# Linear attention and two feed-forward layers in one kernel: running products on (-im, re, im) words, state products in 32-column tiles, a third place for the accumulators' copies, shared places for squares

## The chip, the core and the metric

The kernel runs on one core of a Trainium2 chip. TensorE (PE in the profile) does the matrix products, VectorE (DVE) and ScalarE (ACT) the elementwise work, SyncE (SP) starts the transfers. Each of these engines works off its own queue in order. The metric is the time of one execution on the device in microseconds; the smaller the better.

## The reference, cut to what matters

```python
def _attn_ref(q, k, v, a_re, a_im):          # (4, 8, 768, 48) each
    mag = np.sqrt(a_re * a_re + a_im * a_im)
    scale = np.minimum(mag, 0.999) / (mag + 1e-06)
    a_re_n, a_im_n = (a_re * scale, a_im * scale)
    for t in range(S):
        S_re, S_im = a_re_n*S_re - a_im_n*S_im + k v^T, a_re_n*S_im + a_im_n*S_re
        y[:, :, t] = einsum('bhd,bhde->bhe', q[:, :, t], S_re)

def _moe_ref(x, w_in, w_out):                # 3072 x 384, d_ff 2048
    h = x @ w_in
    return (h * (1.0 / (1.0 + np.exp(-1.702 * h)))) @ w_out

def _moe2_ref(x, w_gate, w_val, w_out):      # d_ff 1536
    g = x @ w_gate
    return (g * (1.0 / (1.0 + np.exp(-g))) * (x @ w_val)) @ w_out

# result: _moe2_ref(_moe_ref(attention's y as 3072 x 384))
```

A linear attention with a complex decay for each key dimension and time step, for 4 batches and 8 heads, then two feed-forward layers over the 3072 tokens. The weights come as 64-bit floats and are converted in the kernel.

## The kernel before

**Attention.** The 768 steps of a batch are cut into chunks of 128, and two chunks make a *unit*: 4 batches x 3 units = 12 units, numbered from 0. For a unit the decays (`u.p`, 128 partitions x real and imaginary part x 768 words) are loaded (`load_a`), squared and summed (`decays`: `sq`, `m2`), brought to scale with a reciprocal root (`root`, ScalarE's Ln and Exp, another function table than the one for Gelu), and multiplied into `u.p` (`scale_pair`). `products` then makes running products over time in place: within each group of 8 steps one complex product after another (`cmul`: one multiply of 4 x 96 words into `sp`, a subtract and an add of 96 words each, lines 390, 397, 399; seven such steps a unit), then over groups of 4 and again 4 (`bq`, `hh`), over the chunks (`G`), and last the prefixes `e` are multiplied into all words (`prod`, line 454). `queries` and `keys` multiply q by the running product and k by its inverse (`inverse`, again Ln and Exp), write them to memory and `load_heads` reads them back by heads (`sq`, `sk`). `turns` transposes the keys on TensorE (`kt`, `kn`). `heads` makes for each chunk the masked scores (`sc`, `at`), the outputs (`y`, 32-column tiles, four of them side by side in the array), and the state's gain (`ds`, line 676: for each of 8 heads one product with 96 columns of weights and 48 moving columns, each in two passes since the words are 32 bits wide); `split_x` leaves y as a high and a low half in `xt`.

**First layer.** `layer_one` multiplies each unit's `xt` with 16 blocks of w_in (`h`, nine products a block, lines 846 to 848), `gelu` follows on ScalarE and VectorE, `layer_one_out` multiplies with w_out into one accumulator of three parts (`acc`), and after a unit's sixteenth block `spill` copies the three parts out on ScalarE (line 944) and sends them to memory (`x2d`). There is one accumulator (`accslots`), so the next unit's first `acc` product waits until the third copy is done. The copies go to tiles named `stage`, of which there are two; a tile is free again when its transfer has landed.

**Second layer.** Blocks of 512 tokens: `pg`, `pv`, silu, `o`. Its weights are converted while the last units of the first layer run.

**What sets the order.** `Plan` is a list scheduler that runs when the kernel is built: each step is a generator that yields events, places (`Slots`) and requests for an engine with an assumed duration; the planner takes what is ready first, with a table of urgencies (`URGENCY`, `EXTRA`, `NEAR`, `W_FIRST`, `SPILL`...), and the instructions go into the engines' queues in that order, which is then fixed. The number of places of each kind is in `BUFS`: four tiles `p`, two tiles `big` (squares, queries, `prod`), one each of `m2`, `x`, `d2`.

Of the kernel before, what the change touches and what calls it, by code (L numbers as in the profile page):

```python
# [185 lines left out]
NEAR = 0.068  # L186
# [7 lines left out]
NEAR0 = [0.129, 0.072]  # L194
# [3 lines left out]
class Attention:  # L198
# [46 lines left out]
    BUFS = dict(p=4, big=2, m2=1, r=1, x=1, d2=1, kr=1, qk=2, v=1, s=1, kn=1, at=2, m=2, sc=2, xt=2, tots=1)  # L245
# [6 lines left out]
    def start(self, units):  # L252

        add = self.plan.add
        for i, (b, c0, n) in enumerate(units):
            u = type("Unit", (), {})()
            u.i, u.b, u.c0, u.n, u.F, u.T, u.t0 = i, b, c0, n, n * self.HD, n * 128, c0 * 128
            u.urgency = {nm: URGENCY[nm] + 10 * i + (EXTRA[i].get(nm, 0) if i < len(EXTRA) else 0) for nm in URGENCY}
            u.near = NEAR0[i] if i < len(NEAR0) else NEAR
            u.ev = {e: Event() for e in ("a", "l", "lv", "q", "k", "v", "m2", "root", "scaled", "prods", "d2", "inv", "qh", "dq", "dk",  # L260
                                        "sq", "sk", "tots", "kn", "x", "phase")}
            u.kn = {}
            u.turned = [Event() for _ in range(n)]
            self.units.append(u)
        for u in self.units:
            last = self.units[u.i - 1] if u.i else None
            for nm, row in (("a", self.load_a(u)), ("l", self.load_qkv(u)), ("d", self.decays(u)),
                            ("p", self.products(u, last)), ("q", self.queries(u)), ("k", self.keys(u)),
                            ("r", self.root(u)), ("i", self.inverse(u)), ("s", self.load_heads(u)), ("t", self.turns(u)), ("h", self.heads(u, last))):
                add(u.urgency[nm], row, near=u.near)  # L270


    def load_a(self, u):
        yield self.slots["p"]
        yield ISSUE2
# [27 lines left out]
    def decays(self, u):  # L303
# [5 lines left out]
        yield slots["m2"]  # L309
# [7 lines left out]
        plan.give(slots["big"])  # L317
        plan.set(u.ev["m2"])
        yield u.ev["root"]
        yield slots["x"]  # L320
        yield act(u.F, more=0.11)
        x = self.tile("x", [128, self.NT, u.T])
# [6 lines left out]
        plan.give(slots["m2"])  # L329
# [7 lines left out]
        plan.give(slots["x"])  # L337
        yield from self.scale_pair(u, u.p, u.r)
        plan.give(slots["r"])
        plan.set(u.ev["scaled"])  # L340
# [30 lines left out]
    def cmul(self, out, x, y, shape):  # L371

        V = self.nc.vector
        n = 1
        for s in shape:
            n *= s
        if len(shape) == 2:
            full = [128, 2] + list(shape)
            for c in range(2):
                yield vec(2 * n)  # L380
                if c == 0:
                    p = self.sb.tile([128, 2, 2, n], F32, tag="sp", name="sp", bufs=2)
# [3 lines left out]
        else:  # L386
            full = [128, 2, 2] + list(shape)
            yield vec(4 * n, 0.3 if n > 48 else 0.0)
            p = self.sb.tile([128, 2, 2, n], F32, tag="sp", name="sp", bufs=2)
# [11 lines left out]
    def products(self, u, last):  # L401
# [5 lines left out]
        pf = u.p.rearrange("p e j (b r) -> p e (j b) r", r=8)  # L407
# [3 lines left out]
        p7 = pf[:, :, :, 7].rearrange("p e (i k) -> p e i k", k=4)  # L411
# [34 lines left out]
        h = g * 16 // n  # L446
        for c in range(n):
            yield slots["big"]
            pv = pf[:, :, cols(c, h)]
            for i in range(2):  # L450
                yield vec(16 * h)
                if i == 0:
                    prod = self.tile("big", [128, 2, 2, h, 8], name="prod")
                V.tensor_tensor(out=prod[:, i], in0=eb[:, i:i + 1, cols(c, h), None].to_broadcast([128, 2, h, 8]), in1=pv,
                                op=ALU.mult)
            yield from self.add_parts(pv, prod, 8 * h)
            plan.give(slots["big"])
        plan.set(u.ev["prods"])
# [71 lines left out]
    def keys(self, u):  # L530
# [3 lines left out]
        yield slots["d2"]  # L534
# [4 lines left out]
        u.d2 = self.tile("d2", [128, self.NT, u.T])  # L539
        V.scalar_tensor_tensor(out=u.d2, in0=sq[:, 0], scalar=1 / BIG / 2 ** 64, in1=sq[:, 1], op0=ALU.max, op1=ALU.add)  # L540
        plan.give(slots["big"])
# [6 lines left out]
        plan.give(slots["d2"])  # L548
# [75 lines left out]
    def heads(self, u, last):  # L624
# [12 lines left out]
        for c in range(u.n):  # L637
# [87 lines left out]
URGENCY = dict(a=-2808.9, d=-847.7, p=-2094.7, r=-3052.8, i=4533.3, q=1516.2, k=-385.1, t=-1239.2, h=76.9, g=-110.3, s=3227.3, l=-328.4, m=-5154.4, x=-1279.9)  # L725
RUSH = 3154.3
RUSH2 = -1700.0
EXTRA = [dict(a=-2098.5, d=-2358.9, p=1710.8, r=-2037.7, i=-2834.0, q=-3757.0, k=-2737.4, t=2298.5, h=973.7, g=-1739.2, s=3534.0, l=8424.0, m=-93.5, x=-1732.5), dict(a=-1805.4, d=1780.9, p=-1232.5, r=-16347.3, i=5601.4, q=-10544.3, k=1608.0, t=-2254.4, h=-1967.0, g=-7019.6, s=-12442.9, l=-9458.0, m=-2831.4, x=3813.5), dict(a=6291.4, d=11280.8, p=-1463.1, r=7217.9, i=-10027.3, q=3231.8, k=2532.1, t=-10835.3, h=-6846.7, g=-312.0, s=-4214.7, l=6684.3, m=-11385.8, x=-3197.1), dict(a=2012.2, d=4387.5, p=299.7, r=-1602.7, i=-86.2, q=6261.4, k=1243.8, t=-1886.3, h=-1311.3, g=-11850.9, s=-3015.3, l=10131.5, m=-5199.2, x=-7519.5), dict(a=-3194.7, d=-6390.0, p=-96.6, r=-3467.8, i=1530.6, q=2540.9, k=-2099.8, t=-5418.7, h=-2426.8, g=-2422.7, s=-767.9, l=-3000.5, m=-5411.6, x=1182.2), dict(a=-1050.3, d=-144.2, p=806.6, r=1424.0, i=139.9, q=-166.2, k=3312.5, t=856.6, h=458.2, g=-4074.4, s=-362.2, l=4171.4, m=-99.2, x=393.5), dict(a=-7427.0, d=5500.1, p=594.0, r=-3662.6, i=725.5, q=-7111.1, k=615.3, t=778.1, h=416.6, g=2162.2, s=-112.0, l=-593.1, m=-1297.8, x=1878.2), dict(a=111.4, d=5462.3, p=1433.9, r=-4618.4, i=24.5, q=3526.1, k=2232.0, t=1785.0, h=-462.5, g=-670.7, s=-71.3, l=-2330.6, m=-2800.1, x=-2443.0), dict(a=-523.3, d=-1120.5, p=-1956.2, r=583.7, i=-4090.9, q=-3868.4, k=-2787.2, t=-4123.6, h=-7130.2, g=1607.9, s=-71.9, l=1329.4, m=-748.8, x=332.7), dict(a=3903.2, d=4589.9, p=1692.7, r=1460.9, i=2272.8, q=1521.7, k=-692.3, t=185.5, h=477.9, g=-6354.1, s=49.3, l=5191.9, m=-1557.4, x=2485.8), dict(a=1214.6, d=-838.8, p=335.0, r=2129.7, i=3251.8, q=-1710.9, k=-2147.3, t=-560.4, h=150.2, g=2186.9, s=1499.3, l=1080.2, m=-2407.0, x=-1150.2), dict(a=-355.1, d=3117.9, p=4624.6, r=-5461.8, i=586.7, q=2689.3, k=-6.4, t=-1989.6, h=-3324.0, g=-682.7, s=4777.1, l=9171.0, m=684.6, x=-1889.2)]
UNITS = [(b, c, 2) for b in range(4) for c in (0, 2, 4)]
W_FIRST, W_STEP = 2068.1, 12.097  # L730
# [3 lines left out]
SPILL = -2740.5  # L734
# [7 lines left out]
def chunked(ctx, tc, keep, dram, q, k, v, a_re, a_im, w_in, w_out, w_gate, w_val, w_out2, out):  # L742
# [31 lines left out]
    stage, rough, junks, wslots = Slots(2), Slots(ROUGH), Slots(1), Slots(2 * F1)  # L774
# [163 lines left out]
    def spill(u, acc):  # L938
        N = u.T
        for c in range(KT):  # L940
            yield stage
            yield act(N, more=-0.05)
            x2 = raw.tile([128, N], F32, tag="stage", name="x2", bufs=2)
# [377 lines left out]
```

## Time and profile before

| | us |
|---|---|
| median of 3 runs (1146.59 to 1150.03) | 1147.72 |
| the profiled execution | 1151.18 |
| its span, first to last instruction | 1149.5 |
| PE busy | 1060.9 (92%) |
| DVE busy | 729.6 (63%) |
| ACT busy | 557.1 (48%) |
| mean granted TensorE clock | 0.962 |

A profile holds one execution. Views used here: the busy time of each engine in stretches of the span (with the granted clock), the table of who waited for whom, the instructions in order of time, and the groups by line. In a row of instructions in time, the first number is the start in microseconds from the span's start, the second the time until the last of the row's instructions ended, then engine, line, operation, result and sources, shapes, and the count; in brackets the idle time of the engine before it, with what ended it. An instruction of DVE or ACT overlaps the next one's start by some tenths of a microsecond, so what it costs its engine is read from start to start.

### The profile page before, as it was taken

Reading aid. Unit: us, or ns where it says so; the run is one execution under the profiler, and the core shown is the slowest. Engines: PE = TensorE matmul, PEld = TensorE weight load, DVE = VectorE, ACT = ScalarE, POOL = GpSimd, SP = SyncE. Lnnn points to the kernel's source line nnn. Section 1 sums busy time; section 2 is a strip of 40 time slices with the busy share of each in tenths; the row PEclk is TensorE's granted clock in tenths of the full one; section 3 lists DMA queues with packets and bytes.
Section 4 is the critical chain, followed back from the end, with each engine's and each line's share of the span. In section 5 each row is a group of like instructions: output and inputs, shape, how many; then the busy total and the mean of one; then the engine's idle time right before and its main releaser. Section 6 shows DMA issues by size and latency. Waiting matters only on the chain.

```text
span 1149.5 us, 19994 instructions
## 1 busy us (share of the span) xinstructions
PE 1060.9 (92%) x7968; PEld 968.7 (84%) x7968; DVE 729.6 (63%) x1646; ACT 557.1 (48%) x1297; POOL 7.5 (1%) x23
## 2 busy tenths in 40 slices
PE   2549988999999999989999999999999999999996
PEld 0228878899999999889999998888888888888885
DVE  6899999999989986898962899432232222312221
ACT  8897565853575547644453999221121222211211
POOL 2000000000000000000000000000000000000000
PEclk9759998999999999899999999999999999999998
DMA  9750634326634246014633680110010010000000
GB/s 335 254 151 29 153 97 124 101 71 189 171 100 113 87 112 179 15 60 107 165 96 81 203 302 23 28 38 17 1 55 1 15 42 1 28 1 1 29 1 30
DMA packets 92182, 103.60 MB, mean 90 GB/s; under 512 B 4785, under 2 KB 86194, under 8 KB 92082
## 3 DMA queue, kind: packets, MB, share of 16 engines
q1 hardware_dynamic: 92082, 102.26, 30.9%
q8 instruction: 64, 1.05, 0.4%
q14 instruction: 36, 0.29, 0.1%
HBM read 73.93 MB, written 28.31 MB: 89 GB/s over the span
## 4 chain that ended last, share of the span: by engine, by line
PE 74%; DVE 11%; DMA 9%; ACT 4%; issue 1%; SPq 1%; DVEq 0%; ACTq 0%
PE o L1070 4%; PE o L1071 4%; PE o L1072 4%; PE pg L847 4%; PE acc L846 4%; PE h L846 4%; PE pv L847 4%; PE pv L846 4%; PE pg L848 4%; PE pg L846 4%; PE pv L848 4%; PE acc L847 4%; PE acc L848 4%; PE h L848 4%; PE h L847 4%; PE sc L616 4%
## 5 line engine op out<-in xcount | busy, mean ns | idle before, releaser
L1040 DVE TENSOR_TENSOR s<-s,pv 128x512 f32<-128x512 f32 x72 | 49.5, 687 | 243.0 <-PE pv L848 241.8
L846 PE MATMUL acc<-gs,w 128*128 128x256 f32 x576 | 169.4, 294 | 14.8 <-ACT x L944 14.8
L846 PE MATMUL h<-xt,w 128*128 128x256 f32 x576 | 169.1, 294 | 4.9 <-ACT g L902 4.9
L847 PE MATMUL acc<-gs,w 128*128 128x256 f32 x576 | 166.2, 289 | 0.3 <-DVE gs L908 0.3
L848 PE MATMUL acc<-gs,w 128*128 128x256 f32 x576 | 166.0, 288 | 0.0
L848 PE MATMUL h<-xt,w 128*128 128x256 f32 x576 | 164.7, 286 | 0.5 <-ACT w L836 0.5
L847 PE MATMUL h<-xt,w 128*128 128x256 f32 x576 | 164.7, 286 | 0.1
L900 ACT ACTIVATE gs<-h 128x256 fp32r<-128x256 f32 x192 | 74.1, 386 | 151.3 <-PE h L848 150.5
L846 PEld LDWEIGHTS acc<-gs,w 128*128 128x128 f32 x576 | 113.6, 197 | 15.8 <-ACT x L944 15.6
L1037 ACT ACTIVATE s<-pg 128x512 f32<-128x512 f32 x72 | 43.1, 599 | 166.8 <-PE pg L848 166.8
L846 PEld LDWEIGHTS h<-xt,w 128*128 128x128 f32 x576 | 112.6, 196 | 8.0 <-ACT g L902 6.6
L847 PEld LDWEIGHTS acc<-gs,w 128*128 128x128 f32 x576 | 113.7, 197 | 0.6 <-DVE gs L908 0.5
L848 PEld LDWEIGHTS acc<-gs,w 128*128 128x128 f32 x576 | 113.6, 197 | 0.0
L847 PEld LDWEIGHTS h<-xt,w 128*128 128x128 f32 x576 | 112.5, 195 | 0.3 <-DVE xt L719 0.3
L848 PEld LDWEIGHTS h<-xt,w 128*128 128x128 f32 x576 | 112.1, 195 | 0.7 <-ACT w L836 0.7
L908 DVE TENSOR_TENSOR gs<-g,gs 128x256 fp32r<-128x256 f32 x192 | 81.0, 424 | 49.5 <-ACT g L902 48.8
L1045 ACT CAST p<-s 128x512 fp32r<-128x512 f32 x72 | 44.8, 622 | 133.5 <-DVE s L1040 133.4
L1070 PE MATMUL o<-w,p 128*128 128x384 f32 x288 | 97.2, 338 | 0.0
L1071 PE MATMUL o<-w,p 128*128 128x384 f32 x288 | 97.2, 337 | 0.0
L1072 PE MATMUL o<-w,p 128*128 128x384 f32 x288 | 97.2, 337 | 0.0
L847 PE MATMUL pg<-xs,w 128*128 128x512 f32 x216 | 85.1, 394 | 0.0
L847 PE MATMUL pv<-xs,w 128*128 128x512 f32 x216 | 84.7, 392 | 0.0
(137 smaller groups left out, 2316.6 us busy)
## 6 DMA issues: line engine op xcount, KB each, us to landing
words<-in_moe_w_out_dram SPq DMA_DIRECT2D x28, 384.0 KB, 8.4
dq<-qh SPq DMA_DIRECT2D x24, 384.0 KB, 4.1
sq<-dq SPq DMA_DIRECT2D x24, 384.0 KB, 6.7
dk<-p SPq DMA_DIRECT2D x24, 384.0 KB, 5.0
sk<-dk SPq DMA_DIRECT2D x24, 384.0 KB, 5.1
words<-in_moe_w_in_dram SPq DMA_DIRECT2D x16, 384.0 KB, 8.5
p<-in_a_re_dram SPq DMA_DIRECT2D x12, 384.0 KB, 3.8
p<-in_a_im_dram SPq DMA_DIRECT2D x12, 384.0 KB, 4.6
```

The costliest lines, as they stand in the source:

```text
L616: T.matmul(sc[:, h], u.sk[:, 4 * g + h, cols(c)], u.sq[:, 4 * g + h, cols(c)], start=True, stop=True)
L846: T.matmul(out, w[:, 0, ws], xh, start=start, stop=False)
L847: T.matmul(out, w[:, 0, ws], xl, start=False, stop=False)
L848: T.matmul(out, w[:, 1, ws], xh, start=False, stop=stop)
L900: A.activation(gs[:, 0], h, AF.Gelu_apprx_sigmoid)
L908: V.tensor_tensor(out=gs[:, 1], in0=g, in1=gs[:, 0].bitcast(F32), op=ALU.subtract)
L1037: A.activation(s, gv[0], AF.Silu)
L1040: V.tensor_tensor(out=s, in0=s, in1=gv[1], op=ALU.mult)
L1045: A.copy(p2[:, 0], s)
L1070: T.matmul(os[i], p2[:, 0, cols(i)], w[:, 0], start=f == 0, stop=False)
L1071: T.matmul(os[i], p2[:, 0, cols(i)], w[:, 1], start=False, stop=False)
L1072: T.matmul(os[i], p2[:, 1, cols(i)], w[:, 0], start=False, stop=f == F2 - 1)
```

## The change

Four edits and a new table of urgencies.

1. **Running products.** Scaled decays are no longer written back into `u.p` but into a tile `tri` (`u.w`) of three words for each element, (-im, re, im); VectorE writes re and im, ScalarE copies -im. One step is then a multiply of 384 words with (re, im) and (-im, re) as pairs, and a single add of 192 words. The last multiply (`prod`) reads `tri` and writes a new `u.p`. `sp` has one tile instead of two.
2. **State products.** Each of the 8 heads' `ds` products becomes three with 32 columns, to three places of the array.
3. **Spill.** `stage` has three tiles instead of two.
4. **Places.** `m2`, `x` and `d2` are halves of the `big` tile that holds the squares, which is given back later; `big` has three tiles, `p` three instead of four. `load_a` waits for the unit before and for the products of the third unit before. Scaling a unit waits for the products of the one before, since there is one `tri`.

```diff
-    BUFS = dict(p=4, big=2, m2=1, r=1, x=1, d2=1, kr=1, qk=2, ...)
+    BUFS = dict(p=3, tri=1, big=3, r=1, kr=1, qk=2, ...)
     def load_a(self, u):
+        if u.i:
+            yield self.units[u.i - 1].ev["al"]
+        if u.i >= 3:
+            yield self.units[u.i - 3].ev["jp"]
         yield self.slots["p"]
...
-        u.m2 = self.tile("m2", [128, self.NT, u.T])
+        x, u.m2 = sq[:, 0], sq[:, 1]
...
-        yield from self.scale_pair(u, u.p, u.r)
+        plan.give(slots["big"])
+        if u.i:
+            yield self.units[u.i - 1].ev["prods"]
+        yield slots["tri"]
+        yield vec(2 * u.F, 0.54)
+        u.w = self.tile("tri", [128, u.F, 3])
+        V.tensor_tensor(out=u.w[:, :, 1:3].rearrange("p n e -> p e n"), in0=u.p.rearrange("p e j t -> p e (j t)"),
+                        in1=u.r.rearrange("p j t -> p (j t)")[:, None].to_broadcast([128, 2, u.F]), op=ALU.mult)
         plan.give(slots["r"])
+        plan.give(slots["p"])
+        yield act(u.F, 0.45)
+        A.activation(u.w[:, :, 0], u.w[:, :, 2], AF.Copy, scale=-1.0)
...
         for r in range(1, 8):
-            yield from self.cmul(pf[:, :, :, r], pf[:, :, :, r], pf[:, :, :, r - 1], [g * 16])
+            yield vec(g * 64)
+            x = w[:, :, r, 1:3]
+            x = bass.AP(x.tensor, x.offset, [x.ap[0], x.ap[1], (-1, 2), (1, 2)])
+            s = sb.tile([128, g * 16, 2, 2], F32, tag="sp", name="sp", bufs=1)
+            V.tensor_tensor(out=s, in0=w[:, :, r - 1, 1:3, None].to_broadcast([128, g * 16, 2, 2]), in1=x, op=ALU.mult)
+            yield vec(g * 32, 0.06)
+            V.tensor_tensor(out=w[:, :, r, 1:3], in0=s[:, :, 0], in1=s[:, :, 1], op=ALU.add)
...
-                yield thin(1.36)
+                yield thin(0.75)
...
-                    T.matmul(ds[:, hs], u.kn[c][:, h].rearrange("p e d -> p (e d)"), self.vp[:, c, h, :D], start=True, stop=True)
+                    for q in range(0, 2 * D, 32):
+                        T.matmul(ds[q:q + 32, hs], u.kn[c][:, h].rearrange("p e d -> p (e d)")[:, q:q + 32],
+                                 self.vp[:, c, h, :D], start=True, stop=True)
...
-URGENCY = dict(a=-2808.9, d=-847.7, p=-2094.7, r=-3052.8, i=4533.3, ...)
+URGENCY = dict(a=915.1, d=564.3, p=-972.3, r=3272.2, i=69.7, ...)
...
-    stage, rough, junks, wslots = Slots(2), Slots(ROUGH), Slots(1), Slots(2 * F1)
+    stage, rough, junks, wslots = Slots(3), Slots(ROUGH), Slots(1), Slots(2 * F1)
```

How the order moves, at three places. TensorE, the second chunk of one of the last units: outputs `y` (sources `vp`, the values, and `M`, the state), then the state products `ds`, then the first layer's products. Before:

```order
L663 MATMUL y<-at,vp 32x128 x4
L663 MATMUL y<-sq,M_130 32x128 x4
L676 MATMUL ds<-vp,kn 96x48 x8
L846 MATMUL acc<-gs,w 128x256
L847 MATMUL acc<-gs,w 128x256
```

After, at the corresponding place:

```order
L684 MATMUL y<-at,vp 32x128 x4
L684 MATMUL y<-sq,M_130 32x128 x4
L698 MATMUL ds<-vp,kn 32x48 x24
L869 MATMUL h<-xt,w 128x256
L870 MATMUL h<-xt,w 128x256
```

Eight products of 96 columns have become 24 of 32 columns, at the same place of the queue.

ScalarE, the copies of unit 6's accumulator (`x<-acc`) among Gelu (`gs`, `g`), the halves of y (`xt`), the table loads and the reciprocal root of another unit (`r<-m`, `r<-r`). Before:

```order
L944 COPY x_5990<-acc 128x256
L944 COPY x_5994<-acc 128x256
L717 ACTIVATE xt,flags<-y 128x3x128
L97 ACT_TABLE_LOAD
L355 ACTIVATE r<-m_5950 128x768
L356 ACTIVATE r<-r 128x768
L944 COPY x_6020<-acc 128x256
```

After, the same unit (`kn` are transposed keys, `hh` is a small copy within the running products):

```order
L967 COPY x_6062<-acc 128x256
L618 COPY kn<-kt 128x8x48
L439 COPY hh<-bq 128x12
L967 COPY x_6080<-acc 128x256
L923 ACTIVATE gs<-h 128x256
L925 ACTIVATE g<-h 128x256
L967 COPY x_6092<-acc 128x256
```

The third copy stands four places behind the second before, with a table load and a reciprocal root between them, and two places behind it now, with the Gelu of one block between them.

VectorE near the start, the last steps of unit 0's running products between the conversion of weights (`r<-words`). Before:

```order
L390 TENSOR_TENSOR sp<-p 128x384
L809 TENSOR_SCALAR r<-words 128x384
L397 TENSOR_TENSOR p<-sp 128x96
L812 SCALAR_TENSOR_TENSOR r<-words,r 128x384
L399 TENSOR_TENSOR p<-sp 128x96
```

After:

```order
L425 TENSOR_TENSOR sp<-tri 128x384
L835 SCALAR_TENSOR_TENSOR r<-words,r 128x384
L427 TENSOR_TENSOR tri<-sp 128x96x2
```

A step is two instructions instead of three. Up to the first masked scores VectorE's queue holds 14 such steps and two scalings (`scale_pair`, or the one into `tri`) in both orders.

## Rows read from the trace of the kernel before

**Rows 1.** Busy time by stretches: PE, PEld, DVE, ACT, POOL; clock; DMA.
```profile
50.00:75.00 25.00, 10.69 (x19) 4.58 (x20) 25.00 (x55) 23.91 (x67) 0.00 (x0) 0.50 0.32 89
...
250.00:275.00 25.00, 25.00 (x265) 24.63 (x264) 23.86 (x54) 14.68 (x34) 0.00 (x0) 1.00 0.74 201
...
725.00:750.00 25.00, 25.00 (x122) 22.00 (x121) 7.90 (x20) 4.89 (x8) 0.00 (x0) 1.00 0.12 33
```

**Rows 2.** Waits of PE from 85 to 625 us: total, times, longest.
```profile
PE acc L846 <- ACT x L944: 14.8, 4, 8.0
PE sc L616 <- DMA sk<-dk: 4.6, 4, 1.7
```

**Rows 3.** In time, PE: unit 1's ds with its successor; two pieces of y.
```profile
151.26 1.56 PE L676 MATMUL ds<-vp,kn 128*96 128x48 f32 x16
152.65 0.51 PE L595 MATMUL kt<-ident,p 128*128 128x128 f32 x3
...
190.61 0.16 PEld L663 LDWEIGHTS y<-at,vp 128*32 128x32 f32 x8
...
191.41 0.29 PE L663 MATMUL y<-sq,M 96*32 96x128 f32 x4
```

**Rows 4.** Line 663's instructions: shortest, median and longest in ns, first and last start.
```profile
L663 PEld LDWEIGHTS y<-at,vp x768: 106/109/113, 91.5 to 625.3; 128*32 128x32 f32 x192
...
L663 PE MATMUL y<-sq,M x640: 270/272/297, 98.1 to 625.6; 96*32 96x128 f32 x160
```

**Rows 5.** The chain that ended last, in time: outputs y of one chunk.
```profile
190.69 1.90 PE y L663 x64
```

**Rows 6.** In time, ACT: copies of the accumulators of units 0, 6 and 7.
```profile
172.19 0.68 ACT L944 COPY x<-acc 128x256 f32<-128x256 f32 x2
...
176.90 0.35 ACT L944 COPY x<-acc 128x256 f32<-128x256 f32 x1
...
473.02 1.28 ACT L97 ACT_TABLE_LOAD   x1
474.31 0.85 ACT L355 ACTIVATE r<-m 128x768 f32<-128x768 f32 x1
...
475.94 0.36 ACT L944 COPY x<-acc 128x256 f32<-128x256 f32 x1
...
512.92 0.65 ACT L944 COPY x<-acc 128x256 f32<-128x256 f32 x2 [1.28 <-PE acc L848]
516.46 0.37 ACT L944 COPY x<-acc 128x256 f32<-128x256 f32 x1 [2.89 <-DMA x2d<-x]
```

**Rows 7.** Busy time in two of four stretches behind such waits, columns as in Rows 1.
```profile
177.30:181.90 4.60, 4.59 (x21) 4.59 (x22) 4.53 (x7) 0.48 (x1) 0.00 (x0) 0.50 0.85 163
...
516.90:519.80 2.90, 2.90 (x13) 2.90 (x14) 2.87 (x9) 1.15 (x4) 0.00 (x0) 0.50 1.07 385
```

**Rows 8.** In time, DVE: one step of the running products between conversions.
```profile
72.67 0.85 DVE L390 TENSOR_TENSOR sp<-p 128x384 f32<-128x384 f32 x1
73.44 0.55 DVE L812 SCALAR_TENSOR_TENSOR r<-words,r 128x384 int32<-128x384 int32 x1
73.91 0.33 DVE L397 TENSOR_TENSOR p<-sp 128x96 f32<-128x96 f32 x1
74.07 0.55 DVE L815 SCALAR_TENSOR_TENSOR r<-words,r 128x384 int32<-128x384 int32 x1
```

**Rows 9.** Groups by line: busy us, mean ns of one, idle before.
```profile
L345 DVE TENSOR_TENSOR p<-p,r 128x1536 f32<-128x1536 f32 x12 | 21.1, 1758 | 0.0
```

**Rows 10.** In time, DVE: first prefix multiplies of units 9 and 10.
```profile
496.25 0.95 DVE L454 TENSOR_TENSOR prod<-e,p 128x768 f32<-128x768 f32 x1
...
533.18 0.95 DVE L454 TENSOR_TENSOR prod<-e,p 128x768 f32<-128x768 f32 x1
```

**Rows 11.** The chain that ended last, in time: first scores of units 2 and 11.
```profile
187.83 1.79 PE sc L616 x16
...
613.75 1.79 PE sc L616 x16
```

More of the change, by code (lines that the diff above doesn't have):

```diff
@@ L185 @@
 ISSUE = ("S", 0.48)
-NEAR = 0.068
+NEAR = 0.091
 SWITCH = 1.3
@@ L193 @@
 TURN = 1018.0
-NEAR0 = [0.129, 0.072]
+NEAR0 = [0.107, 0.059]
 ISSUE2 = ("S", 0.96)
@@ L243, in __init__ @@
         self.done = Event()
-    BUFS = dict(p=4, big=2, m2=1, r=1, x=1, d2=1, kr=1, qk=2, v=1, s=1, kn=1, at=2, m=2, sc=2, xt=2, tots=1)
+    BUFS = dict(p=3, tri=1, big=3, r=1, kr=1, qk=2, v=1, s=1, kn=1, at=2, m=2, sc=2, xt=2, tots=1)
     PARTS = 2
@@ L259, in start @@
             u.near = NEAR0[i] if i < len(NEAR0) else NEAR
-            u.ev = {e: Event() for e in ("a", "l", "lv", "q", "k", "v", "m2", "root", "scaled", "prods", "d2", "inv", "qh", "dq", "dk",
+            u.ev = {e: Event() for e in ("a", "al", "jp", "l", "lv", "q", "k", "v", "m2", "root", "scaled", "prods", "d2", "inv", "qh", "dq", "dk",
                                         "sq", "sk", "tots", "kn", "x", "phase")}
@@ L273, in load_a @@
     def load_a(self, u):
+        if u.i:
+            yield self.units[u.i - 1].ev["al"]
+        if u.i >= 3:
+            yield self.units[u.i - 3].ev["jp"]
         yield self.slots["p"]
+        self.plan.set(u.ev["al"])
         yield ISSUE2
@@ L328, in decays @@
         V.scalar_tensor_tensor(out=u.r, in0=u.m2, scalar=3.0, in1=u.r, op0=ALU.subtract, op1=ALU.mult)
-        plan.give(slots["m2"])
         yield act(u.F)
@@ L446, in products @@
         h = g * 16 // n
+        yield slots["p"]
+        plan.set(u.ev["jp"])
         for c in range(n):
             yield slots["big"]
-            pv = pf[:, :, cols(c, h)]
             for i in range(2):
@@ L452, in products @@
                 if i == 0:
[L453 to L456, printed above, removed]
+                    prod = self.tile("big", [128, 2, h, 8, 2], name="prod")
+                if i == c == 0:
+                    u.p = self.tile("p", [128, 2, NT, u.T])
+                    pf = u.p.rearrange("p e j (b r) -> p e (j b) r", r=8)
+                V.tensor_tensor(out=prod[:, i], in0=eb[:, i, cols(c, h), None, None].to_broadcast([128, h, 8, 2]),
+                                in1=w[:, cols(c, h), :, 1:3], op=ALU.mult)
+            yield from self.add_parts(pf[:, :, cols(c, h)], prod.rearrange("p i h r e -> p i e h r"), 8 * h)
             plan.give(slots["big"])
+        plan.give(slots["tri"])
         plan.set(u.ev["prods"])
@@ L533, in keys @@
         yield slots["big"]
-        yield slots["d2"]
         yield act(2 * u.F)
@@ L538, in keys @@
         yield vec(u.F)
-        u.d2 = self.tile("d2", [128, self.NT, u.T])
+        u.d2 = sq[:, 1]
         V.scalar_tensor_tensor(out=u.d2, in0=sq[:, 0], scalar=1 / BIG / 2 ** 64, in1=sq[:, 1], op0=ALU.max, op1=ALU.add)
-        plan.give(slots["big"])
         plan.set(u.ev["d2"])
@@ L547, in keys @@
         V.scalar_tensor_tensor(out=u.kr, in0=u.d2, scalar=2.0, in1=u.kr, op0=ALU.subtract, op1=ALU.mult)
-        plan.give(slots["d2"])
+        plan.give(slots["big"])
         yield u.ev["k"]
@@ L721, in split_x @@
         plan.set(turned)
[L725 to L728, printed above, removed]
@@ L729 @@
 UNITS = [(b, c, 2) for b in range(4) for c in (0, 2, 4)]
-W_FIRST, W_STEP = 2068.1, 12.097
+W_FIRST, W_STEP = 1114.5, 8.203
 LAG = 3
@@ L733 @@
 EARLY = 32
-SPILL = -2740.5
+SPILL = -1300.2
 LARGE = 2.0 ** 40
@@ L942, in spill @@
             yield act(N, more=-0.05)
-            x2 = raw.tile([128, N], F32, tag="stage", name="x2", bufs=2)
+            x2 = raw.tile([128, N], F32, tag="stage", name="x2", bufs=3)
             A.copy(x2, acc[:, c, :N])
```

17 lines of the change are left out of this document (8 added, 9 removed).

## The prediction

> **What bounds the kernel now.** I read the busy time by stretches first. In [rows 1] the kernel has three stages: at 50 to 75 us DVE is full (25.00 of 25 us) and PE, at clock 0.50, waits for the first units and the converted weights; from 250 us on PE is full at clock 1.00; at 725 us PE is full with the second layer while DVE and ACT are mostly idle. The change touches nothing of the third stage, so whatever it gives comes from an earlier start of PE, from PE's own work, or from PE's stalls in the middle. So I went to PE's waits in the middle [rows 2]: the largest entry by far is the first product into the accumulator waiting for the copies of the unit before, 14.8 us in four pieces, the longest 8.0; next the keys' transfer with 4.6 us. What follows such a wait is seen in [rows 7]: the work behind it runs at a granted clock of 0.50, the lower of its two levels (1.2 of 2.4 GHz), after each of the four idle pieces.
>
> **State products.** Before, the 16 passes of one chunk's ds take from 151.26 to 152.65 us, where the next kind of product starts: 1.39 us, 0.087 us a pass [rows 3]. A pass loads 96 columns of weights and streams 48; since y streams 128 columns in little more time (below), I take the load as what paces ds, 0.9 ns a column. The outputs y show what 32-column tiles do. A chunk's 64 passes take 1.90 us [rows 5], so a round of four tiles, with 128 columns streamed, takes 0.119 us. Eight of their loads, of 109 ns each [rows 4], begin and end within 0.16 us [rows 3]: their starts lie within 0.05 us, 7 ns apart, where loads in single file at 0.9 ns a column would be 29 ns apart. So loads to different tiles overlap. The new ds are 24 products in two passes, 16 rounds of three tiles. A round streams 48 columns (0.119 x 48/128 = 0.045 us) while it loads 32 (0.029): 16 x 0.045 = 0.71 us, and I take 0.75 with the start, a gain of 0.64. There are 20 such pieces (each chunk but the last of each of four batches), all on PE, where they stand at the same place of the queue: 20 x 0.64 = **12.8 us**. Bounds: loads alone, 16 x 0.029 = 0.46 us, would give 18.6; loads in single file, 48 x 0.029 = 1.39, give 0.
>
> Four products of y, 272 ns each [rows 4], begin and end within 0.29 us [rows 3], so their starts are some 6 ns apart. The Trainium skill ("TensorE: Matmul & The Clock Gate", section "Wait — 56ns, not 53.3ns?") says that starts never come closer than about 25 ns however small a product is, which speaks against this edit: 48 passes would be an estimated 1.2 us, a gain of 3.8 us instead of 12.8. The trace differs from it where the products go to different tiles, and the trace decides; what is left of the doubt is in rival (a).
>
> **The third place for the copies.** With two places the third copy waits until the first one's transfer has landed: 2.89 us of idle ACT in unit 7; where other work was put into the gap, it runs first, as in unit 6 (a table load, Ln and Exp ahead of the copy at 475.94) and in unit 0, whose copies run from 172.19 to 176.90 us [rows 6]. Three copies in a row would take 0.9 us (the first two 0.65 to 0.68, the third's 0.36 overlapping). The new order puts them in a row only in some units; mostly the Gelu of one block stands ahead of the third. I went through the eleven handovers in the new queues, with durations of the old trace. Where PE has about 3 us or more of other products between the accumulator's last and next use, nothing waits. Six are left. In unit 0 a table load (1.28), Ln, Exp and a square (0.85 each) still stand between the copies [rows 6], some 5 us in all against one block of other products on PE (nine, about 1 us), so I expect 3.9 us of wait. In five more, 1.8 to 2.3 us stand against 1 to 1.7: 0.5 to 1.0 each, about 4 together. The waits become 8 us instead of 14.8: 6.9 gained. The slow clock: the four stretches hold 4.59, 5.98, 5.95 and 2.90 us of work at 0.50 (the first and the last stand in [rows 7]), and half of these 19.4 us is lost, 9.7. Waits of 1 us should not bring it; unit 0's may cost the 2.3 it costs now. Gained: 7.4. Together **14 us**. Bounds: all gone, 24.5; or the waits only move to other units, 0.
>
> **Running products.** From start to start a step costs DVE 0.77 us for its multiply (72.67 to 73.44) and 0.16 for each of two small ones (73.91 to 74.07), 1.10 in all; an operation on 384 dense words beside it costs 0.47 (73.44 to 73.91) [rows 8]. The new multiply reads pairs of neighbours instead of single words 32 bytes apart: between 0.47 and 0.77, and I take 0.47, since each pair is used twice; the add of 192 words between 0.24 (half of the dense 384) and 0.37 (half of the old multiply), and I take 0.32, two old small ones. A step saves 0.31 us (bounds 0 to 0.4). Against that the scaling of 1536 words, 1.76 us [rows 9], now writes pairs of words 12 bytes apart one by one: between the old price and double; the planner books 0.54 more, which I take. Net for a unit 7 x 0.31 - 0.54 = 1.6 us of DVE. ACT gets a copy of 768 words for each unit, between 0.85 (dense, the Ln of [rows 6]) and double; I take 1.2. On the path this counts only where DVE sets the end, ahead of the first scores. There both orders hold 14 steps and two scalings: 14 x 0.31 - 2 x 0.54 = 3.3 us. ACT, nearly as full (23.91 of 25 us, [rows 1]), gets 2.4 more there, so I take **2 us** (bounds -3 to 4). Later DVE's saving lies beside PE's work and ACT has room (14.68 of 25, [rows 1]).
>
> **Other places.** One `sp` instead of two costs nothing on an engine that works in order. Fewer p and the later release of `big` lengthen a chain, rival (b); in the sum they stand at nothing, since PE's waits for keys are 4.6 us [rows 2] and I leave those as they are.
>
> **The sum.** 12.8 + 14 + 2 = 28.8 us off the profiled execution of 1151.2 (its span of 1149.5 and 1.7 around it) gives 1122.4. That execution lies 3.5 us above the median of 1147.7, so on the median's scale 1118.9; I say 1119.
>
> **Rivals.**
> (a) *The 32-column passes come in single file.* Then ds gains 0, 1132. For it: y's average of 0.030 us a pass would fit a single file too [rows 5]; against: the overlapping loads and products of [rows 3]. With a floor between product starts, as the skill's page has it, 1128.
> (b) *One `tri` makes the units a serial loop, slower than before.* Scaling now waits for the products of the unit before, and the copy of -im stands behind it, so scaling (2.3) and copy (1.2) join the loop from one unit's prefix multiply to the next one's. The shortest such distance that I saw is 496.25 to 533.18, 36.9 us [rows 10], so 40.4 with both. PE takes a unit every (613.75 - 187.83)/9 = 47.3 us now [rows 11], and some 45 by my forecast. Below that the loop is hidden; above it every microsecond counts for nine units, and from about 48.2 on the kernel is slower than before. At 49, for which contention on a DVE that is busy 23.86 of 25 us [rows 1] would have to add 9 us, it is 1119 + 9 x 4 = 1155.
> (c) *The spill's waits move and don't shrink*, since the orders of PE and ACT are rigid and a Gelu ahead of a third copy waits for PE itself: the 14 are lost, 1133.
> (d) *No change*: (a) and (c) together, with a start made later by ACT's extra copies: 1143 to 1149.
>
> **How the numbers follow.** The forecast, 1108 to 1127, has 0.60; (a) 0.08; (c) 0.14; (d) 0.05; (b) 0.08; and a better case 0.05, with all waits of the spill and their slow clock gone and ds paced by loads alone: 1119 - 10.5 - 5.8 = 1103. The range takes in the better case, (a), and (c) with the bad bounds of the start and a part of ds: 1101 to 1140. What a measurement can tell from no change is about 0.3%, 3.4 us, so faster means below 1144.3: forecast, (a), (c), the better case and little of (d), 0.87; slower is (b) and a part of (d), 0.09; the same 0.04.
>
> **What would show it.** ds in 0.75 us from its first product to the next kind, right; 1.2 or more, (a). Waits of `acc` for the copies of 8 us in six pieces, the longest 3 to 4, with one stretch at clock 0.50 behind them, right; about 15 at other units, (c). A step's multiply on DVE near 0.56 us busy instead of 0.85. PE's first unit 2 us earlier. If PE's waits for the keys' transfer grow from 4.6 us to tens, (b). I would be wrong altogether if PE came to wait for something that hardly shows now, such as Gelu behind the new copies of -im on ACT.

## The result and the profile after

The changed kernel takes **1130.26 us** (median of 4 runs, 1129.83 to 1131.85), the kernel before beside it 1147.26 (4 runs, 1146.59 to 1150.03): ratio 0.985, 95% interval 0.983 to 0.987, so 17 us faster. The forecast was 1119, the range 1101 to 1140. The profiled execution of the changed kernel took 1130.28 us with a span of 1128.5, that of before 1151.2 with 1149.5: 20.9 us between the two traces, of which the sum had 28.8. The 1130 lies in the range, but above the forecast's own 1108 to 1127.

The busy time by stretches, columns PE, PEld, DVE, ACT, POOL (each with its instructions), granted clock, DMA share, GB/s, against [rows 1]:

```profile
50.00:75.00 25.00, 7.74 (x15) 3.40 (x15) 25.00 (x46) 23.10 (x61) 0.00 (x0) 0.50 0.41 120
250.00:275.00 25.00, 24.32 (x275) 23.78 (x276) 23.16 (x63) 18.94 (x46) 0.00 (x0) 1.00 0.74 190
725.00:750.00 25.00, 25.00 (x122) 22.05 (x121) 8.03 (x11) 6.57 (x10) 0.00 (x0) 1.00 0.04 16
```

The picture has not changed: DVE is full in the first stage, PE in the other two, and ACT has 4 us more in 25 of the middle. PE's waits from 85 to 625 us (total, times, longest), against [rows 2]:

```profile
PE acc L869 <- ACT x L967: 11.1, 5, 7.1
PE h L869 <- ACT g L925: 9.4, 11, 2.5
PE h L869 <- ACT w L859: 1.2, 1, 1.2
...
PE sc L637 <- DMA sk<-dk: 1.1, 1, 1.1
...
PE acc L869 <- ACT tots L527: 0.8, 1, 0.8
```

Of the kernel before, [rows 2] lack Gelu's row:

```profile
PE h L846 <- ACT g L902: 4.2, 5, 1.5
```

The wait for the copies went from 14.8 us to 11.1 (11.9 with the 0.8 put down to `tots`, a small copy of ACT, which is a wait of the next unit's first accumulation too), that for the keys from 4.6 to 1.1, and that for Gelu from 4.2 to 9.4. All waits that the view lists add up to 28.9 us before and to 28.9 after: **PE waits as long as it did**. What was gained is in PE's own work and in its clock. One chunk of unit 1 in time, PE, for [rows 3]:

```profile
142.34 0.40 PE L684 MATMUL y<-sq,M 96*32 96x128 f32 x8
142.56 0.86 PE L698 MATMUL ds<-vp,kn 128*32 128x48 f32 x48
143.35 0.39 PE L869 MATMUL acc<-gs,w 128*128 128x256 f32 x1
```

From the first ds to the next kind of product it is 0.79 us, where it was 1.39. Over all 20 pieces 27.6 us became 17.3 (16 of them 0.79; the one at 577.8 us waits inside for kn, 0.36 us, and takes 1.44; behind the one at 583.6 the next product waits 0.60 us for the low half in xt, 1.53 with it), and from the last start of y to the first of ds it is 0.09 us instead of 0.20, another 2.2: 12.5 us together. Eight products of 96 columns are 16 records here and 24 of 32 columns are 48, so each takes two passes; that this is because the words are 32 bits wide is not shown, since the transposes of the keys, words of 32 bits too, are one record each (120 of 128 x 128 for 20 chunks of six). For the clock, the same columns for three hundreds of the middle, before and then after:

```profile
125.00:225.00 100.00, 87.97 (x883) 83.67 (x883) 94.15 (x224) 62.15 (x132) 0.00 (x0) 0.94 0.46 115
225.00:325.00 100.00, 98.01 (x981) 95.98 (x980) 90.71 (x244) 47.01 (x119) 0.00 (x0) 0.97 0.54 145
...
425.00:525.00 100.00, 93.99 (x902) 92.39 (x902) 81.22 (x176) 65.29 (x135) 0.00 (x0) 0.95 0.35 96
```

```profile
125.00:225.00 100.00, 87.51 (x998) 83.59 (x998) 91.14 (x213) 65.15 (x138) 0.00 (x0) 0.95 0.52 132
225.00:325.00 100.00, 96.68 (x1136) 94.88 (x1137) 90.44 (x229) 59.65 (x137) 0.00 (x0) 1.00 0.43 115
...
425.00:525.00 100.00, 96.59 (x1093) 94.52 (x1092) 89.74 (x208) 67.05 (x144) 0.00 (x0) 1.00 0.45 119
```

Over the five hundreds from 125 to 625 us the granted clock lacks 16 us of full speed before (0.94, 0.97, 0.98, 0.95, 1.00) and 5 after (0.95, then 1.00): after, the lower level is granted only behind unit 0's wait. So at most 11 us of the difference are from the clock. What the ds (12.5) and the start (0.8) leave of the 20.9 is 7.6, or some 7 when the waits that stand in these two as well are counted once; it is a remainder, not a measurement.

The second column to see is DVE: 90 to 94 of 100 us are busy in the first two of these hundreds, before and after. The prediction used such a share in the middle (23.86 of 25 us, [rows 1]) for rival (b) alone. On DVE itself (busy us, mean ns of one, idle before) the steps of the running products and the scaling now read:

```profile
L425 DVE TENSOR_TENSOR sp<-tri 128x384 f32<-128x384 f32 x84 | 48.3, 575 | 0.9
L427 DVE TENSOR_TENSOR tri<-sp 128x192 f32<-128x192 f32 x84 | 35.9, 428 | 1.1
L345 DVE TENSOR_TENSOR tri<-p,r 128x1536 f32<-128x1536 f32 x12 | 27.6, 2300 | 0.0
```

The scaling went from 1758 ns [rows 9] to 2300, the 0.54 that was taken; a step is 575 + 428 ns, 1.00 us, where the same view of before has 891 + 2 x 344, 1.58. These are durations, and an instruction starts before the one ahead of it has ended. From start to start, as the prediction counted, one step among other work costs 0.75 us after (217.44 to 217.91 for the multiply, 218.78 to 219.06 for the add) against 1.10 in [rows 8]: 0.35 saved, where 0.31 was expected.

### The profile page after: what moved, and what is told of

Same layout as the page of the kernel before. It is cut to its first block, busy times and chain, and to the rows that moved or that the text cites. A ratio compares the mean times of both kernels' runs of the same rounds, so it can differ in the third digit from the quotient of the medians.

```text
span 1128.5 us, 21202 instructions
## 1 busy us (share of the span) xinstructions
PE 1042.4 (92%) x8608; PEld 949.4 (84%) x8608; DVE 704.4 (62%) x1562; ACT 570.6 (51%) x1311; POOL 7.7 (1%) x23
## 3 DMA queue, kind: packets, MB, share of 16 engines
q8 instruction: 69, 1.13, 0.4%
## 4 chain that ended last, share of the span: by engine, by line
PE 76%; ACT 10%; DVE 7%; DMA 5%; issue 1%; SPq 0%; DVEq 0%; ACTq 0%
PE h L869 5%; PE acc L869 5%; PE o L1093 4%; PE o L1094 4%; PE o L1095 4%; PE pg L870 4%; PE h L871 4%; PE h L870 4%; PE pv L870 4%; PE pg L871 4%; PE pv L869 4%; PE pg L869 4%; PE acc L870 4%; PE pv L871 4%; PE acc L871 4%; PE sc L637 4%
## 5 line engine op out<-in xcount | busy, mean ns | idle before, releaser
L869 PE MATMUL acc<-gs,w 128*128 128x256 f32 x576 | 167.8, 291 | 11.8 <-ACT x L967 11.1
L870 PE MATMUL acc<-gs,w 128*128 128x256 f32 x576 | 164.4, 285 | 0.9 <-DVE gs L931 0.9
L871 PE MATMUL acc<-gs,w 128*128 128x256 f32 x576 | 164.1, 285 | 0.0
L869 PEld LDWEIGHTS h<-xt,w 128*128 128x128 f32 x576 | 111.2, 193 | 15.9 <-ACT g L925 13.2
L869 PEld LDWEIGHTS acc<-gs,w 128*128 128x128 f32 x576 | 111.6, 194 | 14.1 <-ACT x L967 12.1
L870 PEld LDWEIGHTS acc<-gs,w 128*128 128x128 f32 x576 | 111.7, 194 | 1.4 <-DVE gs L931 1.3
L871 PEld LDWEIGHTS acc<-gs,w 128*128 128x128 f32 x576 | 111.5, 194 | 0.0
L870 PEld LDWEIGHTS h<-xt,w 128*128 128x128 f32 x576 | 111.3, 193 | 0.0
L871 PEld LDWEIGHTS h<-xt,w 128*128 128x128 f32 x576 | 111.2, 193 | 0.0
```

Source lines behind the costliest of these rows:

```text
L869: T.matmul(out, w[:, 0, ws], xh, start=start, stop=False)
L870: T.matmul(out, w[:, 0, ws], xl, start=False, stop=False)
L871: T.matmul(out, w[:, 1, ws], xh, start=False, stop=stop)
```

## Experiments

Theory T1: the gain is the ds tiles and the third place; the words give nothing on the path. Rivals are named in each expectation. The runs were on several chips, so the ratios to the kernel before on the same chip are compared; one thousandth is 1.15 us.

**The ds tiles, done alone and undone alone.** Both edits leave every engine's order as it is.

```diff
-                    T.matmul(ds[:, hs], u.kn[c][:, h]..., self.vp[:, c, h, :D], ...)
+                    for q in range(0, 2 * D, 32):
+                        T.matmul(ds[q:q + 32, hs], u.kn[c][:, h]...[:, q:q + 32], self.vp[:, c, h, :D], ...)
```

> The kernel before with the ds products in three 32-column tiles and nothing else; the cost in the planner's list stays 1.36, so every engine's order is the one of before. Theory T1 (the gain of the change is the ds tiles, about 12 us, and the third place for leaving accumulators, about 10 us; the words, the shared places and the new numbers give nothing net): ds falls from 1.38 to 0.79 us a piece, 20 pieces, and the gap ahead of it from 0.20 to 0.09; 11 to 13 us faster than before, ratio 0.989 to 0.990. Theory T2 (the gain is the new order and the lighter VectorE; ds is absorbed by the waits next to it): 0 to 4 us, ratio 0.997 to 1.000.

> The changed kernel with ds back in 96-column products; cost in the list stays 0.75, order of every engine unchanged. T1: 11 to 13 us slower than the changed kernel, about 1142 us, ratio to before 0.995. T2: 0 to 4 us slower, about 1132 us, ratio 0.986.

Alone: 1138.06 us, ratio 0.992 (0.990 to 0.995), 9 us gained by the medians and 11.8 from span to span. Undone: 1143.41, ratio 0.997 (0.995 to 0.998), 13 us lost. A piece takes 0.79 us in the first and 1.38 in the second. In both, PE's waits for the copies are those of the kernel they were made from (14.8 and 11.1 us). The clock stays with the order as well: over the five hundreds it lacks 14 us of full speed with the tiles alone (16 before) and 7 with the tiles undone (5 in the changed kernel). So the tiles are worth 9 to 13 us, and by more than half of the 17 they are the result.

**The third place, with an order made anew by the old numbers.** In the kernel before the room for it was made by `sp` with one buffer.

```diff
-    stage, rough, junks, wslots = Slots(2), Slots(ROUGH), Slots(1), Slots(2 * F1)
+    stage, rough, junks, wslots = Slots(3), Slots(ROUGH), Slots(1), Slots(2 * F1)
...
-            x2 = raw.tile([128, N], F32, tag="stage", name="x2", bufs=2)
+            x2 = raw.tile([128, N], F32, tag="stage", name="x2", bufs=3)
```

> The kernel before with the ds tiles and three places for leaving accumulators; the room for the third place comes from one buffer fewer for VectorE's intermediate products (tag sp, 2 to 1), which only VectorE writes and reads. No words, no shared places, numbers of before; the planner, which is told of the third place, orders anew. T1: as fast as the changed kernel or faster, 1124 to 1132 us, ratio 0.980 to 0.986. T2: 1134 to 1140 us, ratio 0.989 to 0.994.

> The changed kernel with two places for leaving accumulators, in the tile and in the planner's list; the planner orders anew. T1: the copies wait for a transfer again in some units, PE waits for them 5 to 8 us more and 3 to 5 more clock windows fall: 6 to 14 us slower than the changed kernel, 1136 to 1144 us. T2 (the waits of before came from its order, not from the missing place): within 3 us of the changed kernel.

The kernel before with tiles and third place: 1146.56 us, ratio 0.999 (0.997 to 1.000), slower than with the tiles alone and outside of both expectations. The changed kernel without the place: 1154.76, ratio 1.006 (1.005 to 1.008), 24 us lost, more than either expected. PE's waits in the first of them:

```profile
PE acc L846 <- ACT x L944: 16.3, 7, 3.9
PE h L846 <- ACT g L902: 14.4, 12, 2.5
```

The planner took the same urgencies and, with one more place, made another order: seven units wait for the copies instead of four, and Gelu comes late for 14.4 us (4.1 with the tiles alone). The numbers fit one list of work and no other, so these two runs tell as much of the order as of the place. From here on the order was either held fixed or found anew.

**The third place with the order held.** Only the tile's buffers change (the second line of the diff), not what the planner is told.

> The kernel before with three buffers behind the leaving accumulators, the planner still told of two, so every engine's order is the one of before; room comes from one buffer fewer for VectorE's intermediate products. T1 (the third place pays by itself, since the third copy no longer waits for a transfer): units 6 and 7 lose their waits of 2.7 and 2.9 us and one to three low clock windows with them, units 0 and 1 keep theirs, which stand behind other work in ScalarE's queue: 4 to 8 us faster than before, ratio 0.993 to 0.9965. T3 (the place pays only where the order is made anew for it, since the planner had already put the third copy late): 0 to 2 us, ratio 0.998 to 1.000.

> The changed kernel with two buffers behind the leaving accumulators, the planner still told of three, so every engine's order is the one of the changed kernel. The third copy then waits on ScalarE for the first one's transfer in most of the 12 units. [...] T3: 0 to 4 us slower.

Added to the kernel before it gives nothing, as T3 had it: 1148.52 us, ratio 1.001 (0.999 to 1.003). Taken from the changed kernel it costs 12.5 us, where T3 had 0 to 4: 1142.89, ratio 0.996 (0.994 to 0.998), with waits for the copies of 18.1 us instead of 11.1, and a clock that lacks 14 us of full speed in the five hundreds instead of 5. Why nothing in the first? Unit 7 shows it. PE's longest wait from 510 to 570 us, in the kernel before and then with the third buffer:

```profile
PE acc L846 <- ACT x L944: 2.9, 1, 2.9
```

```profile
PE acc L847 <- DVE gs L908: 2.8, 1, 2.8
```

The wait for the copies is gone, and one of the same length for the low parts of Gelu, a DVE subtraction, has taken its place. In time, with the third buffer, ACT and then DVE:

```profile
513.72 0.93 ACT L944 COPY x<-acc 128x256 f32<-128x256 f32 x3 [1.29 <-PE acc L848]
514.80 0.38 ACT L900 ACTIVATE gs<-h 128x256 fp32r<-128x256 f32 x1 [0.15 <-PE h L848]
517.84 0.38 ACT L902 ACTIVATE g<-h 128x256 f32<-128x256 f32 x1 [2.66 <-DVE gs L908]
```

```profile
513.94 0.94 DVE L552 SCALAR_TENSOR_TENSOR kr<-kr,k 128x768 f32<-128x768 f32 x1
514.81 0.32 DVE L399 TENSOR_TENSOR p<-sp 128x96 f32<-128x96 f32 x1
514.98 1.74 DVE L345 TENSOR_TENSOR p<-p,kr 128x1536 f32<-128x1536 f32 x1
516.65 0.83 DVE L390 TENSOR_TENSOR sp<-p 128x384 f32<-128x384 f32 x1
517.40 0.41 DVE L908 TENSOR_TENSOR gs<-g,gs 128x256 fp32r<-128x256 f32 x1
```

The same subtraction in the kernel before:

```profile
516.63 0.45 DVE L908 TENSOR_TENSOR gs<-g,gs 128x256 fp32r<-128x256 f32 x1
```

The three copies now run in a row from 513.72 on. But DVE works from 506 to 517 us without a gap through keys, queries and a running product, and the subtractions stand behind these in its order. In the kernel before, where ACT was named as the last releaser, the product that had waited for it started at 516.88 us; the subtraction, which the next product reads, ended at 517.08, 0.2 us later. With or without the copies' wait PE could not have gone on much earlier.

**The old steps on the words.** Each step is again three DVE instructions, at the same points of every engine's order.

```diff
-            V.tensor_tensor(out=s, in0=w[:, :, r - 1, 1:3, None]..., in1=x, op=ALU.mult)
+            V.tensor_tensor(out=s.rearrange("p a i e -> p i e a"), in0=w[:, :, r - 1, None, 1:3].rearrange(...)...,
+                            in1=w[:, :, r, 1:3, None].rearrange(...)..., op=ALU.mult)
             yield vec(g * 32, 0.06)
-            V.tensor_tensor(out=w[:, :, r, 1:3], in0=s[:, :, 0], in1=s[:, :, 1], op=ALU.add)
+            V.tensor_tensor(out=w[:, :, r, 1], in0=s[:, :, 0, 0], in1=s[:, :, 1, 1], op=ALU.subtract)
+            V.tensor_tensor(out=w[:, :, r, 2], in0=s[:, :, 0, 1], in1=s[:, :, 1, 0], op=ALU.add)
```

> The changed kernel with the steps of the running products back as three VectorE instructions of the old strides (384 products, a subtract and an add), on the same words and in the same places of every engine's order: about 0.89 + 2 x 0.34 us in place of 0.58 + 0.43, so 0.5 to 0.6 us more for each of 84 steps, some 47 us of VectorE. T1 (the words give nothing on the path): within 4 us of the changed kernel. T2 (VectorE's relief gives a part of the gain): 8 to 20 us slower.

1189.87 us, ratio 1.038 (1.035 to 1.041): **60 us** slower than the changed kernel, far outside of both. Part of it is that the instructions take longer than was expected:

```profile
L425 DVE TENSOR_TENSOR sp<-tri 128x384 f32<-128x384 f32 x84 | 93.4, 1112 | 0.9
L427 DVE TENSOR_TENSOR tri<-sp 128x96 f32<-128x96 f32 x168 | 53.6, 394 | 1.1
```

By these durations a step is 1.90 us instead of 1.00, 75 us in 84 steps. From start to start one step among other work is 1.50 us (240.78 to 241.80 and 242.67 to 243.15) instead of 0.75, some 63 us in 84, and 60 reach the end. The last accumulation of unit 0 ends at 182.8 us (166.4 in the changed kernel), of unit 4 at 406.2 (365.1), of unit 8 at 606.5 (546.5), and stays 60 later. So under this order DVE has hardly any slack up to unit 8. In PE's time the 60 show as longer waits (63 us from 85 to 625 us instead of 28.9) and as a slower clock behind them (0.86, 0.97, 0.95, 0.97 and 0.97 in the five hundreds, 28 us of full speed instead of 5). The prediction's sentence that DVE's saving lies beside PE's work fails for a given order.

**No copies of -im.** The copy on ACT is left out, and the running products read im in place of -im.

```diff
-        A.activation(u.w[:, :, 0], u.w[:, :, 2], AF.Copy, scale=-1.0)
...
-            x = bass.AP(x.tensor, x.offset, [x.ap[0], x.ap[1], (-1, 2), (1, 2)])
+            x = bass.AP(x.tensor, x.offset, [x.ap[0], x.ap[1], (0, 2), (1, 2)])
```

> The changed kernel without the copies of -im on ScalarE (12 of 1.29 us); the running products then read im where -im stood, so that their values are other ones. Nothing else moves. If PE waits for Gelu because of these copies (the prediction's own condition for being wrong): the 9.4 us of waits for Gelu fall to about 4, and 5 to 9 us are gained. If they stand behind table loads, Ln, Exp and squares, which the new order has put ahead of them: 0 to 2 us.

The whole took 9683.0 us, since the kernel computes everything again by its general branch when its own guard finds values such as these; only the first 700 us of the trace, the same work in the same order, bear on the question. PE's waits there, 85 to 625 us:

```profile
PE acc L869 <- ACT x L967: 11.1, 5, 7.1
PE h L869 <- ACT g L925: 10.0, 10, 4.0
```

Waits for Gelu of 10.0 us instead of 9.4, and the last accumulation of units 5 to 11 within 0.03 us of the changed kernel's (the last one at 672.46 and 672.48), though unit 0's was 1.9 us later. So the copies cost nothing on the path, as the second theory had it, and the 9.4 us of waits for Gelu are not theirs.

**Numbers found anew for each version.** The planner's numbers were moved at random in small steps, and a step was kept where the planner's own last product came earlier. This went on twice as long for the first and third version below as for the other two, and each version had one such search; how far another or a longer one would move a time isn't known. Of the code itself the diffs above are all (tiles, third place), and the numbers' begins for the changed kernel with

```diff
-RUSH = 4923.9
+RUSH = 62440.9198
...
-SPILL = -1300.2
+SPILL = -47970.8672
```

The expectations are for the changed kernel, for the kernel before, for the kernel before with tiles and third place (no words, no shared places), and for the changed kernel with two places:

> The changed kernel, with only the planner's numbers (urgencies, rushes, near) new: moved at random by small steps and kept where the planner's own last product came earlier, from 668.8 to 658.3 us. Nothing of the work changes. Every engine's order is another. T1 (PE's remaining waits are a matter of order): the planner's 10 us show on the chip for a good part, 1120 to 1126 us, 4 to 10 faster than the changed kernel. T2 (the planner's times are finer than what it models): 1127 to 1133 us.

> The kernel before with nothing new but the planner's numbers, found in the same way as those of the changed kernel with new numbers (the planner's last product moves from 691.2 to 687.0 us only, where the changed kernel's moved from 668.8 to 658.3). T1 (what made room was the change; numbers alone find little in the kernel before): 0 to 6 us faster than before, ratio 0.995 to 1.000. T2 (most of the gain of the other kernels with new numbers is the search itself): 8 to 15 us faster, ratio 0.987 to 0.993.

> The kernel before with the ds tiles and the third place (one buffer fewer for VectorE's intermediate products), without words, shared places and copies of -im, with numbers of its own found the same way as for the kernel with new numbers (as long a search): planner's last product at 665.3 us instead of 658.3. T1 (the words give nothing on the path, as the prediction had it): as fast as the changed kernel with its new numbers, within 3 us, 1120 to 1126. T2 (VectorE sets the pace through much of the middle, so that the words carry a part of the gain): 5 to 12 us slower than that, 1127 to 1134 us.

> The changed kernel with two places for leaving accumulators, in the tile and in the planner's list, with numbers of its own found the same way (half as long a search): planner's last product at 666.9 us. T1 (the third place is worth about 10 us, as the run with the place taken away under an unchanged order says): 7 to 14 us slower than the changed kernel with new numbers, 1127 to 1136 us. T2 (an order made for two places loses little): 0 to 5 us slower than it.

| version, with its own numbers | median us | ratio | 95% |
|---|---|---|---|
| changed kernel | 1124.28 | 0.978 | 0.975 to 0.981 |
| before | 1142.05 | 0.994 | 0.992 to 0.996 |
| before with tiles and third place | 1126.69 | 0.980 | 0.977 to 0.982 |
| changed kernel with two places | 1141.28 | 0.992 | 0.989 to 0.995 |

The first of these is faster than both kernels and lies in T1's 1120 to 1126. New numbers gave 7 to 8 us by the ratios in the kernel before and in the changed one alike, a little more than T1 had for the former, so the distance between them stays: 0.978/0.994 = 0.984. The third version, without any words, has 0.980 and lies some 2 us behind the first, which the intervals don't tell from none: with an order made for it, the old running products cost next to nothing, within the 3 us of T1. Its DVE is busy 96.19 of 100 us from 125 to 225 us (91.49 in the first version), but its order has put the waits elsewhere:

```profile
PE acc L846 <- ACT x L944: 13.4, 7, 6.8
PE acc L847 <- DVE gs L908: 5.4, 4, 3.0
...
PE h L846 <- ACT g L902: 1.0, 4, 0.4
```

The last row of the table, 17 us behind the first and outside of both expectations, doesn't price the third place. PE's waits there are

```profile
PE acc L869 <- ACT x L967: 16.1, 2, 15.1
```

and 15.1 of them are unit 0: its accumulator is done at 160.32 us, and the first copy, which needs no place to come free, starts at 169.90, behind three table loads, two pairs of Ln and Exp, Gelu and a square of 1536 words in ACT's order. Only the rest can be the place: the third copy stands 5.4 us behind the second (170.99 and 176.38), behind other work, and waits its last 0.36 us for the first one's transfer. An estimate is what tiles and place together give over the tiles: 0.994 to 0.980 is 16 us together, each with its own numbers, and the tiles 9 to 13 with the order held, which leaves 3 to 7 for the place. The run that would show it, the tiles alone with numbers of their own, was not made.

## Why the prediction was right, and where not

The 1130 alone doesn't tell the forecast (1119) from rivals (a) and (c), whose 1128 to 1133 lie nearer to it; the range took them in. The traces and runs tell them apart, term by term.

**State products: right.** Sum 12.8, bounds 0 to 18.6; the traces show 12.5 (10.3 in the pieces and 2.2 ahead of them, which the sum didn't count), and the runs 9 (alone) to 13 (undone). The piece took 0.79 us where 0.75 was worked out from y's rounds. Rival (a) is out. That y's loads start 7 ns apart was the row that decided. The 48 passes in 0.79 us are 16 ns each. The Trainium skill ("TensorE: Matmul & The Clock Gate", section "Wait — 56ns, not 53.3ns?") has product starts no closer than about 25 ns. The trace differs from it for products to different column tiles.

**The third place: its idle time was mis-sized.** 8 us of waits were expected, 3.9 at unit 0 and about 4 in five others, a gain of 6.9; 11.9 were found, a gain of 2.9. The five are there, units 1, 3, 6, 7 and 9, with 0.8 to 1.1 us each (unit 1's is the one put down to `tots`). Unit 0 waits 7.1. ACT's order there, in time:

```profile
167.43 1.51 ACT L316 ACTIVATE sq<-p 128x1536 f32<-128x1536 f32 x1
...
168.90 0.41 ACT L923 ACTIVATE gs<-h 128x256 fp32r<-128x256 f32 x1
...
169.95 0.44 ACT L967 COPY x<-acc 128x256 f32<-128x256 f32 x1
170.41 1.28 ACT L97 ACT_TABLE_LOAD   x1
171.70 0.84 ACT L366 ACTIVATE r<-sq 128x768 f32<-128x768 f32 x1
172.58 0.84 ACT L367 ACTIVATE r<-r 128x768 f32<-128x768 f32 x1
173.33 0.35 ACT L967 COPY x<-acc 128x256 f32<-128x256 f32 x1
173.58 0.84 ACT L325 ACTIVATE sq<-r 128x768 f32<-128x768 f32 x1
...
174.42 0.36 ACT L967 COPY x<-acc 128x256 f32<-128x256 f32 x1
```

The last accumulation starts at 166.38, the next unit's first at 174.83: 8.4 us, of which PE fills 1.4 with other products. From the first copy on it is 4.9, the "some 5 us" of the prediction; the other 3.6 are a square of 1536 words and four blocks' Gelu ahead of the first copy. The step counted what lies between the copies and not what lies ahead of them. With new numbers the same wait is 2.1 us, so it is a matter of order.

**The slow clock: right in size, in part by luck.** 7.4 was expected, with unit 0 alone keeping its stretch; some 7 is what the other terms leave, under a bound of 11, and only unit 0's stretch is left. But the sum gave all of it to the copies. The kernel before has a fifth stretch between 125 and 625 us,

```profile
417.50:420.50 3.00, 3.00 (x16) 3.00 (x15) 3.00 (x6) 0.00 (x0) 0.00 (x0) 0.50 0.09 29
```

and it stands behind 1.67 us of wait for the keys' transfer; the one of 5.98 us of work stands behind 1.45 us for Gelu as well as 1.13 for the copies. Nor are the slow stretches the place's alone: with new numbers and two places the kernel before lacks 5 us of full speed in the five hundreds (0.97, 1.00, 1.00, 0.98, 1.00), as little as the changed kernel.

**Waits for Gelu, left out of the sum, grew by 5.2 us.** The prediction named them as what would make it wrong, but as waits behind the copies of -im, and the run without these shows that they are not the cause. Ahead of the three longest (2.5, 1.9 and 1.3 us) ACT's order has a table load, and ahead of that two squares (of 1536 and 768 words, from 122.85 us on), a conversion that came 2.3 us late from DVE, or Ln and Exp. That these are the cause is read from the order; no run took them away. With its new numbers the changed kernel still waits 10.0 us for Gelu, the kernel before with tiles and third place 1.0, so it is not in the work itself. The gain of 3.5 us at the keys, which were left as they were, pays for a part. Rival (c), waits that move and don't shrink, is thus right for the waits as a whole (28.9 us both times), and wrong in that the clock came back with shorter pieces.

**Running products: near in size by luck, wrong in the reason.** Their start was to give 2 us; PE's first scores came at 87.1 us instead of 87.9, so 0.8. PE's last wait ahead of them is for ACT both times (1.8 us for `junk` before, 1.1 for `w` after), so it isn't shown that DVE set their time. "Later DVE's saving lies beside PE's work" is false for a given order (60 us for some 63 of DVE's time) and nearly true for the best order that was found for either form (some 2 us). Rival (b) has no sign: the wait for the keys fell.

**The scale.** 3.5 us were taken off because the profiled execution of before lay above its median; that of the changed kernel lies at its median. That the sum's waits and slow stretches, read in that execution, already held the 3.5 us would fit this, and isn't shown. With 28.8 expected and 20.9 found between the traces (7.9), this makes the 11 us between 1119 and 1130.

## What to carry to other kernels

Ask of each wait that is to go what would have come next: the 2.9 us of unit 7 had a second releaser 0.2 us behind, on an engine that worked without a gap. Where the order is planned with numbers tuned to one list of work, taking a part out under that order, or planning anew with the old numbers, measures the order (60 us, or 8 us lost by adding a place); compare versions that each have numbers of their own. And a copy's wait in a queue is what stands ahead of the first one as well as what stands between them.

## What the runs showed of the hardware that was not expected

- Products in 32-column tiles follow others in 32-column tiles with less of a pause than 96-column ones did: 0.09 us from the last start of y to the first of ds, 0.20 before and when the tiles are undone.
- The same 384 products on DVE took 575 ns where pairs of neighbours are read and written, 891 in the kernel before (0.85 us for the one in [rows 8]), and 1112 where single words are read 96 bytes apart and written 16 bytes apart.
- The length of a wait did not tell whether a slow stretch follows: one of 1.67 us (keys) had work at 0.50 behind it in the kernel before, one of 2.55 us (Gelu, at 127.26 us) had none in the changed kernel.
- The copy of -im, 768 words 12 bytes apart on ACT, took 1293 ns, where an operation on 768 dense words, Ln, takes 0.85 us [rows 6]; the scaling on DVE that writes at three words took 2300 ns for 1758. The Trainium skill ("SBUF — State Buffer", section "Door 1: The DMA port swizzle (why `[64,N]` ≈ `[32,N]`)") has lines of 16 bytes, and from them that one can stride by up to four fp32 words for free. The trace differs: at three words the copy costs half as much again, with another function than Ln's in it, and the scaling a third more.
